# Loading values by head over all 128 partitions, with the keys of a block taken in the order 7u + n

## The chip, the cores and the metric

The kernel runs on one core of one Trainium2 chip. The metric is the device time of one execution in microseconds (us); lower is better.

## The reference

The program is a sigmoid attention followed by a mixture-of-depths layer. Everything is float32. Cut to what matters:

```python
# q, k, v: (B=8, H=12, S=448, Dh=64)
scores = q @ k.T / sqrt(64) - log(448)         # per batch and head, 448 x 448
attn = 1 / (1 + exp(-scores))                  # no softmax: each weight stands alone
x = (attn @ v), heads side by side             # (8, 448, 768)
score = x @ w_gate                             # one number per token
top = the 128 tokens of a batch with the highest score
out = x;  out[top] += sigmoid(score[top]) * (relu(x[top] @ w1) @ w2)   # w1 768 x 1024, w2 1024 x 768
```

Because each attention weight stands alone and the product with v sums over all keys, the keys of a head may be taken in any order, provided that the rows of v are taken in the same order.

## The kernel before

**Tiling.** The 8 x 12 heads are handled in 24 quads of four heads, and two quads make one of the NS = 12 stages s. A head has 448 tokens, seen as 32 groups of TB = 14 consecutive tokens: token 14t + r, with t the partition within a group of 32 partitions and r from 0 to 13. A quad's q or k therefore fills 128 partitions (4 heads x 32 values of t) with 14 x 64 numbers each, and is loaded by one DMA (`load`, L91). VectorE then turns 32 x 32 blocks (`turn`, L367), so that TensorE finds the head dimension on partitions.

**Slots.** Each stage has NU = 7 slots n. In a slot, `score` (L387) forms the scores of 128 keys (64 of either quad) against all 448 queries, `squash` (L402) applies the sigmoid on ScalarE into an `attn` tile, and `value` (L416) multiplies earlier `attn` tiles with `raw_v` and accumulates in PSUM. The scores run ahead of the values: the values of stage s begin in slot 4 of stage s and end in slot 3 of stage s + 1. In stages 4 to 11 a piece of the mixture-of-depths layer (`block`, L736) is placed between slot 3 and slot 4.

**Which keys a slot takes.** A pair of key columns r lies side by side in `kT`. In `turn` the pairs are (n, n + 7). In stage 0 the pairs are others: `load_first` loads columns 3 to 10 of the keys first (AT = 3), `turn_first` turns pairs such as (3, 9) and (5, 7), and `load_second` brings the values and the remaining columns 0 to 2 and 11 to 13.

**Values.** `load_v` (L189) fills `raw_v`: 32 partitions hold, for one quad and for either the even or the odd member of the pairs, seven columns of four heads. So one stage's values come in four DMAs m, each onto 32 partitions, each with 128 pieces of 1,792 bytes:

```python
def block(x, r, n):
    return bass.AP(tensor=v.tensor, offset=v.offset + (8 * s + 4 * x) * S * Dh + r * Dh,
                   ap=[[TB * Dh, TT], [S * Dh, 4], [1, n * Dh]])
```

Stage 0 is loaded in two parts: first five columns (`load_v(0, True)`, L219), then two (`load_v(0, False)`, L222). In front of the first part stands a one-element `memset` of `raw_v` on VectorE (L205). The DMAs wait for it, so its place in VectorE's order sets when SP may issue them. In stages 1 to 5 the values are issued by SP (L216): `after` calls `load_v(s + 1)` at slot 3 of stage s, and `load_v(1)` in slot 6 of stage 0. From stage 6 on they are issued by ScalarE's queue (L216), `load_v(s)` at slot 3 of stage s itself: from stage 7 on the tile is free only when the values of stage s - 1 are finished, and slot 4 needs it. The `block` of the stage lies between.

**Order.** The kernel writes its order out by hand (`stream`, `slot`, `after`); each engine executes its own instructions in that order. SP issues nearly all loads and stores on one queue, ScalarE the late values on a second, GpSimd the small exchanges and the gathers on a third. `raw_k` has one buffer, so each key load waits until VectorE has turned the keys before it.

Of the kernel before, what the change touches and what calls it, by code (L numbers as in the profile page):

```python
# [17 lines left out]
def kernel(  # L18
# [11 lines left out]
    nc = tc.nc  # L30

    B, H, S, Dh = q.shape
# [3 lines left out]
    P = 128  # L36
    TT = 32
    TB = S // TT
# [5 lines left out]
    NU = 2 * NF + 1  # L44
# [44 lines left out]
    heads, raw_v = {}, {}  # L89

    def load(which, *quads):  # L91

        for i in quads:
            if i >= NQ:
                return
            if which == "q":
                t = heads["q", i] = head.tile([P, TB * Dh], F32, name="qT")
            elif i == 2:
                t = heads["both"][:, TB * Dh:2 * TB * Dh]
            else:  # L100
                t = head.tile([P, TB * Dh], F32, name="raw_k", bufs=1)
            src = q if which == "q" else k
            nc.sync.dma_start(
                out=t, in_=bass.AP(tensor=src.tensor, offset=src.offset + i * 4 * S * Dh,
                                   ap=[[TB * Dh, P], [1, TB * Dh]]))
            heads[which, i] = t

    def load_first():

        raw = {}  # L110
        for i in range(2):
            if i:
                both = heads["both"] = moe.tile([P, 6 * KH * P], F32, name="rows_t")
                raw["k", i] = both[:, :TB * Dh]
            else:
                raw["k", i] = head.tile([P, TB * Dh], F32, name="raw_k", bufs=1)
            raw["q", i] = head.tile([P, TB * Dh], F32, name="qT")
            for which, src, at, n in (("k", k, AT, TB - 2 * AT), ("q", q, 0, TB)):
                heads[which, i] = raw[which, i]
                nc.sync.dma_start(  # L120
                    out=raw[which, i][:, at * Dh:(at + n) * Dh],
                    in_=bass.AP(tensor=src.tensor, offset=src.offset + (i * 4 * S + at) * Dh,
                                ap=[[TB * Dh, P], [1, n * Dh]]))

    def load_second():

        load_v(0, True)
        for i in range(2):
            t = heads["k", i].rearrange("p (r d) -> p r d", d=Dh)
            for r in (0, TB - AT):  # L130
                nc.sync.dma_start(
                    out=t[:, r:r + AT],
                    in_=bass.AP(tensor=k.tensor, offset=k.offset + (i * 4 * S + r) * Dh,
                                ap=[[TB * Dh, P], [Dh, AT], [1, Dh]]))
        load_v(0, False)

    turned = {}

    def turn_first(i, *parts):

        t = heads["k", i].rearrange("p (r e d) -> p e r d", e=2, d=TT)
        if i not in turned:
            turned[i] = head.tile([P, 2, TB, TT], F32, name="kT")
        kt = turned[i]
        for part in parts:
            if part < 2:
                nc.vector.transpose(kt[:, :, 2 * part:2 * part + 2],
                                    t[:, :, AT + part:AT + part + NA + 2:NA + 1])
                nc.vector.transpose(kt[:, :, 2 * (NA + part):2 * (NA + part) + 2],
                                    t[:, :, NA + part:NA + part + 3:2])  # L150
                continue
            for a, r in ((0, 0), (1, TB - AT)):
                nc.vector.transpose(kt[:, :, 4 + a:2 * NA:2], t[:, :, r:r + AT])  # L153

    def spare(n):
        return spares.tile([P, QW], F32, name=f"spare{n}")
# [6 lines left out]
    def chunks(s, n, y):  # L163

        if s:
            return y, n, NU
        alone = n < 2 if y else 1 < n < 4
        if alone:
            return 1 - y, 2 * NA + n % 2, 2
        return y, n - 2 * (y or n > 3), NA  # L170

    def column(s, n, y):

        x, c, step = chunks(s, n, y)
        return c if s or step == NA else c - NA

    NA = NU - 2
    AT = NA - 2
    assert NA + 4 + NA == TB and AT + 8 + AT == TB

    hiddens = {}

    def hidden(p):

        if p not in hiddens:
            hiddens[p] = moe.tile([P, 7 * FH * P], F32, name="hidden")
        return hiddens[p]

    def load_v(s, pairs_too=None):  # L189


        if s >= NS:
            return
        if s == 0 and not pairs_too:
            t = raw_v[s]
        elif s in (1, 3):
            t = moe.tile([P, 6 * KH * P], F32, name="rows_t")[:, :4 * NU * Dh]
        elif s == min(BLOCKS) + 1:
            t = hidden(0)[:, 3 * FH * P:3 * FH * P + 4 * NU * Dh]
        else:  # L200
            t = vals.tile([P, 4 * NU * Dh], F32, name="raw_v")
        if s or pairs_too:
            raw_v[s] = t = t.rearrange("p (h c) -> p h c", h=4)
        if pairs_too:
            nc.vector.memset(t[:1, 0, :1], 0.0)  # L205

        def block(x, r, n):
            return bass.AP(tensor=v.tensor,
                           offset=v.offset + (8 * s + 4 * x) * S * Dh + r * Dh,
                           ap=[[TB * Dh, TT], [S * Dh, 4], [1, n * Dh]])  # L210

        for m in range(4):
            y, odd = divmod(m, 2)
            rows = slice(m * TT, (m + 1) * TT)
            if s:
                (nc.scalar if s > 5 else nc.sync).dma_start(  # L216
                    out=t[rows], in_=block(y, odd * NU, NU))
            elif pairs_too:
                nc.sync.dma_start(out=t[rows, :, :NA * Dh],  # L219
                                  in_=block(y, odd * (NA + 4), NA))  # L220
            else:
                nc.sync.dma_start(out=t[rows, :, NA * Dh:],  # L222
                                  in_=block(1 - y, NA + 2 * odd, 2))

    QW = KH * FH * P
    assert D == 4 * NF * Dh and 4 * NU * Dh <= 6 * KH * P
# [138 lines left out]
    def turn(which, *quads):  # L367


        for i in quads:  # L370
            if i >= NQ:
                return
            t = heads[which, i].rearrange("p (r e d) -> p e r d", e=2, d=TT)
            if which == "q":
                if i > 1:
                    nc.vector.transpose(heads["q", i], heads["q", i])  # L376
                    continue
                heads["q", i] = qt = head.tile([P, TB * Dh], F32, name="qT")
                qt = qt.rearrange("p (e r t) -> p e r t", e=2, t=TT)
                for e in range(2):  # L380
                    nc.vector.transpose(qt[:, e], t[:, e])
                continue
            heads["k", i] = kt = head.tile([P, 2, TB, TT], F32, name="kT")
            for e in range(2):
                nc.vector.transpose(kt[:, e], t[:, e].rearrange("p (a n) d -> p n a d", a=2))  # L385

    def score(s, n, e, pr, out):  # L387

# [27 lines left out]
    def value(s, half, p, n):  # L416


        for r in (2 * half, 2 * half + 1):
            x, c, step = chunks(s, n, half)  # L420
            pr = r % 2 ^ p
            rows = slice(r * TT, (r + 1) * TT)
            at = column(s, n, half)
            if s == 0 and at < NA and r % 2 == 0:
                at = (at + AT) % NA
            at *= Dh
            i = done[s, x, pr] = done.get((s, x, pr), 0) + 1
            for j in range(2):
                nc.tensor.matmul(PO[x][pr][j * Dh:(j + 1) * Dh, :S],  # L429
                                 raw_v[s][rows, 2 * pr + j, at:at + Dh],  # L430
                                 attn[s, pr, n][rows, j, :],
                                 start=((s, x, pr, j) not in done), stop=(i == TB))
                done[s, x, pr, j] = True
# [539 lines left out]
    def after(s, n):  # L973

        if n == NF and s:
            odd = s in FULL[1::2]
# [31 lines left out]
            lend(m, key, place)  # L1008
        if s == 0:
            if n == 0:  # L1010
                turn_first(1, 0)
                load_second()
                turn("q", 1)
                turn_first(1, 1)
                turn_first(0, 2)
                turn_first(1, 2)
                load("k", 2, 3)
                load("q", 2, 3)
            if n == 4:
                turn("k", 2, 3)  # L1020
                gate_weights()
                load("k", 4)
            if n == 5:
                turn("q", 2, 3)
            if n == 6:
                load_v(1)
        if (s, n) in WEIGHTS:
            m, x = WEIGHTS[s, n]
# [81 lines left out]
```

## Time and profile before

| | |
|---|---|
| Median of 3 runs | 434.03 us (432.82 to 434.27) |
| The profiled execution | 434.43 us, of which the span of the profile is 432.6 us and 1.8 us lie around it |
| TensorE busy | 424.7 us (98%) |
| VectorE, ScalarE, GpSimd busy | 281.6, 190.3, 48.0 us |
| DMA moved | 78.64 MB in 114,937 packets, mean 182 GB/s |
| Granted TensorE clock | 1.0 |

The profile gives, for each engine, its busy time; the span in 40 slices with a digit in tenths; the DMA queues with packets, bytes and the share of the time of all 16 DMA engines together; and, by query, who waited for whom and single instructions in order of time. Queue q1 is SP's, q10 is ScalarE's and q0 is GpSimd's. PE is TensorE, DVE VectorE, ACT ScalarE, POOL GpSimd. A busy share of the DMA is a mean over 16 DMA engines: it does not say how evenly they are loaded.

### The profile page before, as it was taken

How to read it: one execution, taken by the hardware profiler on the slowest of the kernel's cores; microseconds unless marked ns; L12 is line 12 of the kernel's file. 1: busy time of each engine (PE TensorE's matmuls, PEld its weight loads, DVE VectorE, ACT ScalarE, POOL GpSimd, SP SyncE). 2: the span in 40 equal slices, each digit the busy share in tenths (PEclk: the TensorE clock that was granted, in tenths of full speed). 3: DMA queues.
4: the chain of work that ended last, by engine and by line, in shares of the span. 5: the costliest groups of instructions: out<-in, count | busy, mean ns of one | idle time of the engine just before them, and what ended most of it. 6: DMA issues, size and time to landing. Idle time of an engine off the chain costs nothing.

```text
span 432.6 us, 14250 instructions
## 1 busy us (share of the span) xinstructions
PE 424.7 (98%) x6324; PEld 254.7 (59%) x6324; DVE 281.6 (65%) x597; ACT 190.3 (44%) x249; POOL 48.0 (11%) x81
## 2 busy tenths in 40 slices
PE   8999999999999999999999999999999999999995
PEld 3455453545666478465447549546545859769952
DVE  4427557583967776976968636755666648983472
ACT  4666656666664633650660651563264330101100
POOL 3000001210210020100302020010020110101001
PEclk9999999999999999999999999999999999999999
DMA  6896747899863997988566887399935981821001
GB/s 191 245 273 178 285 89 155 207 209 251 252 180 74 244 296 186 261 269 204 182 224 184 240 204 152 103 265 277 264 109 116 236 241 36 162 57 77 23 1 73
DMA packets 114937, 78.64 MB, mean 182 GB/s; under 512 B 91420, under 2 KB 100892, under 8 KB 114876
## 3 DMA queue, kind: packets, MB, share of 16 engines
q1 hardware_dynamic: 107948, 62.47, 55.0%
q0 software_dynamic: 3296, 9.54, 7.6%
q10 hardware_dynamic: 3632, 5.74, 5.4%
q8 instruction: 49, 0.80, 0.8%
q14 instruction: 12, 0.10, 0.1%
HBM read 57.25 MB, written 20.48 MB: 180 GB/s over the span
## 4 chain that ended last, share of the span: by engine, by line
PE 93%; DMA 3%; ACT 1%; issue 1%; SPq 1%; DVE 1%; POOLq 0%; ACTq 0%
PE a L397 30%; PE o L429 28%; PE o L616 11%; PE o L680 11%; PE a L616 6%; PE a L680 5%; DMA rows_t<-in_k_dram 1%; DMA raw_k<-in_k_dram 1%; PE o L580 1%; ACT attn L411 1%; DMA out_dram<-xe,idx 1%; SPq L219 0%; PE a L580 0%; POOLq L1105 0%; SPq L120 0%
## 5 line engine op out<-in xcount | busy, mean ns | idle before, releaser
L397 PE MATMUL a<-qT,kT 32*64 32x448 f32 x2624 | 244.9, 537 | 0.9 <-DVE kT L153 0.5
L411 ACT ACTIVATE attn<-a,bias_s 128x896 f32<-128x896 f32 x162 | 161.4, 1007 | 86.1 <-PE a L397 81.7
L429 PE MATMUL o<-attn,raw_v 32*64 32x448 f32 x1952 | 176.6, 537 | 0.1
L397 PEld LDWEIGHTS a<-qT,kT 32*64 32x64 f32 x2624 | 95.6, 131 | 90.3 <-ACT attn L411 52.8
L429 PEld LDWEIGHTS o<-attn,raw_v 32*64 32x64 f32 x1952 | 69.5, 131 | 29.3 <-issue 22.5
L453 DVE STREAM_TRANSPOSE x_b<-o 128x448 f32<-128x448 f32 x48 | 28.1, 626 | 53.6 <-PE o L429 37.3
L429 PE MATMUL o<-attn,rows_t 32*64 32x448 f32 x448 | 41.9, 538 | 0.0
L632 ACT ACTIVATE hidden<-hidden 128x512 f32<-128x512 f32 x12 | 7.5, 630 | 65.8 <-DVE hidden L629 65.8
L629 DVE TENSOR_TENSOR hidden<-o,hidden 128x512 f32<-128x512 f32 x23 | 15.2, 687 | 24.2 <-PE o L616 24.0
L464 DVE TENSOR_REDUCE gate_p<-scr 128x14 f32<-128x448 f32 x48 | 29.8, 621 | 1.7
L461 DVE TENSOR_TENSOR scr<-x_b,wg_b 128x448 f32<-128x448 f32 x48 | 29.5, 615 | 1.1
L385 DVE STREAM_TRANSPOSE kT<-raw_k 128x448 f32<-128x448 f32 x42 | 24.1, 611 | 4.0 <-PE a L397 3.7
L376 DVE STREAM_TRANSPOSE qT<-qT 128x896 f32<-128x896 f32 x22 | 23.8, 1083 | 4.2 <-DMA qT<-in_q_dram 3.5
L616 PE MATMUL o<-rows_t,spare 128*128 128x128 f32 x216 | 25.6, 276 | 0.0
L616 PEld LDWEIGHTS o<-rows_t,spare 128*128 128x128 f32 x216 | 24.8, 192 | 1.4 <-DVE x_b L453 1.4
L680 PE MATMUL o<-spare,hidden 128*128 128x384 f32 x72 | 24.3, 487 | 0.0
L691 DVE SCALAR_TENSOR_TENSOR xe<-o,gate,xe 128x384 f32<-128x384 f32 x29 | 16.6, 612 | 9.7 <-PE o L680 9.6
L519 DVE SCALAR_TENSOR_TENSOR scr<-rep,who,tie 128x448 f32<-128x448 f32 (+1 forms) x28 | 18.9, 677 | 4.9 <-DMA rep<-scores 4.2
L535 POOL DMA_DIRECT2D ranks<-turned x28 | 14.5, 525 | 67.0 <-DVE turned L532 67.0
L429 PEld LDWEIGHTS o<-attn,rows_t 32*64 32x64 f32 x448 | 17.0, 131 | 5.7 <-issue 5.2
L429 PE MATMUL o<-attn,hidden 32*64 32x448 f32 x224 | 20.2, 535 | 0.0
L616 PEld LDWEIGHTS o<-rows_t,w_sb 128*128 128x128 f32 x168 | 19.3, 192 | 1.0 <-DVE x_b L453 0.7
(118 smaller groups left out, 392.7 us busy)
## 6 DMA issues: line engine op xcount, KB each, us to landing
qT<-in_q_dram SPq DMA_DIRECT2D x24, 448.0 KB
out_dram<-x_b SPq DMA_DIRECT2D x32, 336.0 KB
raw_k<-in_k_dram SPq DMA_DIRECT2D x21, 448.0 KB
spare<-sum SPq DMA_DIRECT2D x18, 384.0 KB
sum<-spare SPq DMA_DIRECT2D x8, 768.0 KB
raw_v<-in_v_dram ACTq DMA_DIRECT2D x24, 224.0 KB
w_sb<-in_moe_w_dram SPq DMA_DIRECT2D x6, 768.0 KB
rows_t<-in_v_dram SPq DMA_DIRECT2D x8, 224.0 KB
```

The source lines that it names most:

```text
L376: nc.vector.transpose(heads["q", i], heads["q", i])
L385: nc.vector.transpose(kt[:, e], t[:, e].rearrange("p (a n) d -> p n a d", a=2))
L397: nc.tensor.matmul(out[y * Dh:(y + 1) * Dh, h % 2, :S], kt[d, e, r:r + 2].rearrange("d r t -> d (r t)"), qt[d, e], start=(e == 0), stop=(e ...
L411: nc.scalar.activation(a, psc[:, :, :S], AF.Sigmoid, bias=bias_s, scale=QK_SCALE)
L429: nc.tensor.matmul(PO[x][pr][j * Dh:(j + 1) * Dh, :S], raw_v[s][rows, 2 * pr + j, at:at + Dh], attn[s, pr, n][rows, j, :], start=((s, x, p ...
L453: nc.vector.transpose(x_tiles[b][:, :, 2 * g + pr, :], PO[x][pr][:, :S].rearrange("p (r t) -> p r t", t=TT))
L461: nc.vector.tensor_tensor(out=tmp, in0=x_tiles[b][:, :, hp, :], in1=wg_b[:, hp:hp + 1, :].to_broadcast([P, TB, TT]), op=ALU.mult)
L464: nc.vector.tensor_reduce(out=gate_parts[b][:, :, hp], in_=tmp, axis=AX.X, op=ALU.add)
L519: nc.vector.scalar_tensor_tensor(out=junk[:n], in0=rep[:n], scalar=own, in1=tie[:n], op0=ALU.subtract, op1=ALU.is_gt, accum_out=place_s[:n ...
L616: nc.tensor.matmul(ps[:, f, :n], w((t * FH + f) * P, P), x[:, t, :n], start=(t == 0), stop=(t == KH - 1))
L680: nc.tensor.matmul(ps[:n, :DH], h[:, t, :n], w(t * DH, DH), start=(t == 0), stop=(t == FH - 1))
L691: nc.vector.scalar_tensor_tensor(out=xe[:n, cols], in0=ps[:n, :DH], scalar=st[b]["gate"][:n, 0:1], in1=xe[:n, cols], op0=ALU.mult, op1=ALU ...
```

## The change

1. **Values.** A stage's values are now laid out by key order 7u + n: token 7u + n of a head lies on partition u (64 partitions for each of the two quads) in column n. `load_v` issues one DMA for each of the four heads, onto 128 partitions. The pieces are again 1,792 bytes. On the DRAM side the pattern is two quads, then 64 rows, then 448 numbers; on the SBUF side it is 128 partitions, then 448 numbers. The built program carries them so: `[114688, 2], [448, 64], [1, 448]` against `[1792, 128], [1, 1], [1, 448]` (stride, count). Before, both sides began with a count of 32. For stage 0 the first part has the same form with 320 numbers; the second part is two DMAs of 64 partitions.
2. **Turns of k.** To match, the two members of a pair are interleaved key by key: `by_two` makes each turn of k write with a stride of two numbers.
3. **First keys.** Stage 0 now uses the pairs (n, n + 7) as well. `first_keys` loads columns 3 to 6 and 10 to 13 first (two pieces of 1,024 bytes for each partition, before one of 2,048), then columns 0 to 2 and 7 to 9 in one DMA a quad (before two).
4. **Order.** `load_second` stands before `turn_first(1, 0)` instead of after it. On VectorE the `memset` of `raw_v` comes before the two turns of the second quad's first keys. On SP `load_second` has 8 DMAs instead of 12. The instructions of TensorE, ScalarE and GpSimd keep their number and order, and so do all other DMAs.

```diff
+    def first_keys(i, r, n):
+        t = heads["k", i].rearrange("p (a c) -> p a c", a=2)
+        nc.sync.dma_start(
+            out=t[:, :, r * Dh:(r + n) * Dh],
+            in_=bass.AP(tensor=k.tensor, offset=k.offset + (i * 4 * S + r) * Dh,
+                        ap=[[TB * Dh, P], [NU * Dh, 2], [1, n * Dh]]))
...
     def load_second():
         load_v(0, True)
         for i in range(2):
-            t = heads["k", i].rearrange("p (r d) -> p r d", d=Dh)
-            for r in (0, TB - AT):
-                nc.sync.dma_start(
...
+            first_keys(i, 0, AT)
         load_v(0, False)
...
+    def by_two(t):
+        return t.rearrange("p e (n a) t -> p e n (a t)", a=2).rearrange(
+            "p e n (t a) -> p e n a t", a=2)
...
-        for m in range(4):
-            y, odd = divmod(m, 2)
-            rows = slice(m * TT, (m + 1) * TT)
-            if s:
-                (nc.scalar if s > 5 else nc.sync).dma_start(
-                    out=t[rows], in_=block(y, odd * NU, NU))
...
+        def rows(x, h, n, *dims):
+            return bass.AP(tensor=v.tensor,
+                           offset=v.offset + (8 * s + 4 * x + h) * S * Dh + n * Dh,
+                           ap=[*dims, [NU * Dh, 2 * TT]])
+
+        if s or pairs_too:
+            n = NU if s else NA
+            for h in range(4):
+                src = rows(0, h, 0, [4 * S * Dh, 2])
+                src = bass.AP(tensor=src.tensor, offset=src.offset, ap=[*src.ap, [1, n * Dh]])
+                (nc.scalar if s > 5 else nc.sync).dma_start(out=t[:, h, :n * Dh], in_=src)
+            return
+        for y in range(2):
+            src = rows(1 - y, 0, NA)
+            src = bass.AP(tensor=src.tensor, offset=src.offset,
+                          ap=[*src.ap, [S * Dh, 4], [1, 2 * Dh]])
+            nc.sync.dma_start(out=t[y * Dh:(y + 1) * Dh, :, NA * Dh:], in_=src)
...
-                nc.vector.transpose(kt[:, e], t[:, e].rearrange("p (a n) d -> p n a d", a=2))
+                nc.vector.transpose(by_two(kt)[:, e], t[:, e].rearrange("p (a n) d -> p n a d", a=2))
...
             if n == 0:
+                load_second()
                 turn_first(1, 0)
-                load_second()
                 turn("q", 1)
```

More of the change, by code (lines that the diff above doesn't have):

```diff
@@ L116, in load_first @@
                 raw["k", i] = head.tile([P, TB * Dh], F32, name="raw_k", bufs=1)
+            heads["k", i] = raw["k", i]
             raw["q", i] = head.tile([P, TB * Dh], F32, name="qT")
-            for which, src, at, n in (("k", k, AT, TB - 2 * AT), ("q", q, 0, TB)):
-                heads[which, i] = raw[which, i]
-                nc.sync.dma_start(
-                    out=raw[which, i][:, at * Dh:(at + n) * Dh],
-                    in_=bass.AP(tensor=src.tensor, offset=src.offset + (i * 4 * S + at) * Dh,
-                                ap=[[TB * Dh, P], [1, n * Dh]]))
+            first_keys(i, AT, NU - AT)
+            t = heads["q", i] = raw["q", i]
+            nc.sync.dma_start(
+                out=t, in_=bass.AP(tensor=q.tensor, offset=q.offset + i * 4 * S * Dh,
+                                   ap=[[TB * Dh, P], [1, TB * Dh]]))
     def load_second():
@@ L128, in load_second @@
         for i in range(2):
-            t = heads["k", i].rearrange("p (r d) -> p r d", d=Dh)
-            for r in (0, TB - AT):
[L131 to L134, printed above, removed]
+            first_keys(i, 0, AT)
         load_v(0, False)
@@ L139, in turn_first @@
     def turn_first(i, *parts):
-        t = heads["k", i].rearrange("p (r e d) -> p e r d", e=2, d=TT)
+        t = heads["k", i].rearrange("p (a n e d) -> p e n a d", a=2, e=2, d=TT)
         if i not in turned:
             turned[i] = head.tile([P, 2, TB, TT], F32, name="kT")
-        kt = turned[i]
+        kt = by_two(turned[i])
         for part in parts:
             if part < 2:
[L147 to L150, printed above, removed]
+                for at, n in ((part, AT + part), (NA + part, NA + part)):
+                    nc.vector.transpose(kt[:, :, at], t[:, :, n])
                 continue
-            for a, r in ((0, 0), (1, TB - AT)):
-                nc.vector.transpose(kt[:, :, 4 + a:2 * NA:2], t[:, :, r:r + AT])
+            for a in range(2):
+                nc.vector.transpose(kt[:, :, 2:NA, a], t[:, :, :AT, a])
+    def by_two(t):
+        return t.rearrange("p e (n a) t -> p e n (a t)", a=2).rearrange(
+            "p e n (t a) -> p e n a t", a=2)
     def spare(n):
@@ L178 @@
     AT = NA - 2
-    assert NA + 4 + NA == TB and AT + 8 + AT == TB
+    assert NA + 2 == NU and AT + 4 == NU and TB == 2 * NU
     hiddens = {}
@@ L205, in load_v @@
             nc.vector.memset(t[:1, 0, :1], 0.0)
-        def block(x, r, n):
+        def rows(x, h, n, *dims):
             return bass.AP(tensor=v.tensor,
-                           offset=v.offset + (8 * s + 4 * x) * S * Dh + r * Dh,
-                           ap=[[TB * Dh, TT], [S * Dh, 4], [1, n * Dh]])
-        for m in range(4):
-            y, odd = divmod(m, 2)
-            rows = slice(m * TT, (m + 1) * TT)
-            if s:
-                (nc.scalar if s > 5 else nc.sync).dma_start(
-                    out=t[rows], in_=block(y, odd * NU, NU))
[L218 to L223, printed above, removed]
+                           offset=v.offset + (8 * s + 4 * x + h) * S * Dh + n * Dh,
[12 more added lines that the diff above has]
+            nc.sync.dma_start(out=t[y * Dh:(y + 1) * Dh, :, NA * Dh:], in_=src)
     QW = KH * FH * P
@@ L423, in value @@
             at = column(s, n, half)
-            if s == 0 and at < NA and r % 2 == 0:
+            if s == 0 and at < NA:
                 at = (at + AT) % NA
```

## The prediction

> **What bounds the kernel now.** First the busy table and the slices of the page:
>
> ```profile
> span 432.6 us, 14250 instructions
> PE 424.7 (98%) x6324; PEld 254.7 (59%) x6324; DVE 281.6 (65%) x597; ACT 190.3 (44%) x249; POOL 48.0 (11%) x81
> ...
> DMA  6896747899863997988566887399935981821001
> ...
> q1 hardware_dynamic: 107948, 62.47, 55.0%
> ...
> q10 hardware_dynamic: 3632, 5.74, 5.4%
> ```
>
> TensorE is busy 98% of the span: any gain must come from its 8 us of idle time, and a loss comes from any load that arrives late. The DMA digits say that the 16 engines are far from idle while values are loaded. By stretches (PE, PEld, DVE, ACT, POOL, then clock, DMA share, GB/s):
>
> ```profile
> 6.70:104.00 97.30, 96.68 (x1913) 47.46 (x1895) 53.25 (x122) 64.05 (x76) 6.86 (x11) 1.00 0.80 209
> ...
> 155.00:346.00 191.00, 190.66 (x2800) 114.70 (x2806) 131.01 (x268) 83.54 (x116) 21.44 (x33) 1.00 0.78 205
> ```
>
> The DMA engines are 0.80 and 0.78 busy there, evenly loaded or not, and TensorE still waits for none of them: all loads fit their windows. How wide the windows are, the timeline shows; here stage 9, first ScalarE's queue, then TensorE:
>
> ```profile
> 260.20 0.32 ACTq L216 DMA_DIRECT2D raw_v<-in_v_dram  x1
> ...
> 262.04 0.95 ACTq L216 DMA_DIRECT2D raw_v<-in_v_dram  x2
> ```
>
> ```profile
> 273.26 0.60 PE L397 MATMUL a<-qT,kT 32*64 32x448 f32 x4
> 273.28 0.60 PE L429 MATMUL o<-attn,raw_v 32*64 32x448 f32 x4
> ```
>
> From the first issue to the first use: 13.1 us. Read in the same way, the windows of stages 6 to 11 are 13.0 (155.16 to 168.18), 13.5 (190.81 to 204.32), 10.4 (226.34 to 236.72), 13.1, 13.5 (295.34 to 308.85) and 11.0 (330.85 to 341.88), mean 12.4 us. The DMA view of 256 to 285 us gives what one stage's values cost:
>
> ```profile
> q10 hardware_dynamic: 576, 0.92, 13.3%
> ```
>
> That is 0.133 x 16 x 29 us = 62 us of one engine, or 3.9 us on each of 16. The view of 30 to 35 us shows the pace of a saturated DMA:
>
> ```profile
> DMA  9999989989999999999999999999897637000000
> GB/s 430 401 401 459 459 344 459 459 344 402 430 459 393 397 410 406 373 422 373 410 410 393 442 426 393 393 426 360 328 344 295 246 131 213 16 0 0 0 0 0
> ```
>
> About 410 GB/s at a digit of 9, or 25.7 GB/s for each engine.
>
> **What the skill says.** (1) "DMA: Bandwidth & Descriptors", section "Why a DMA increments its semaphore by 16 and not by 1": a DMA is cut along the slowest dimension with a count over 1 of each side, over the largest number k of engines, at most 16, that divides both counts; each used engine adds one completion write; from SP and ScalarE the lowest-numbered k engines are taken. The trace agrees as far as it can. Queue q10 has 3,632 packets. The code puts on it 24 value DMAs of 128 pieces (3,072), one of 128 rows (128) and four of 4 rows (16): 3,216. The remaining 416 are 25 x 16 + 4 x 4, so a 4-row DMA used 4 engines; had it used 16, there would be 464. That the engines are the lowest ones no run here shows yet. (2) Same page, "Queues, rings and completion order": each engine works a queue's pieces in ring order and takes turns between queues. (3) "SBUF — State Buffer", "Door 1: The DMA port swizzle": 32 partitions reach half of the 16 ports. The trace fits: the values ran at 0.92 MB in 62 us, 15 GB/s for each engine, against 25.7. (4) Same page, same section: SBUF works in lines of 16 bytes and needs two hits in each, so a stride of two 4-byte numbers should be free. No strided turn is in the trace.
>
> **The change, part by part.**
>
> *Values, the part that decides.* The DRAM side now begins with a count of 2 and the SBUF side with 128. By (1), k = 2: every value DMA runs on the same two engines. A set of four is 917,504 bytes, 35.7 us of an engine at 25.7 GB/s, so at least 17.9 us on two. At the old pace of 15 to 17.6 GB/s (10.9% of 16 x 30 us between 150 and 180) it would be 26 to 31 us. Now each half of the partitions has its own ports, so I take the fast end with some cost for pieces: **19 us a set** instead of 3.9, and 13.6 us for stage 0's first part (655,360 bytes).
>
> Over the run: without the values the engines work about 220 us each between 6.7 and 346 us (shares of .80, .75 and .78 by their stretches of 97.3, 51 and 191 us, 265 us, less 45 for 11.7 sets). Two engines then get 220 + 11 x 19 + 14 = 443 us of work in 339 us. They become the bound: +104 us if they never rest, some 30 less if the other pieces run faster once they are no longer in each other's way.
>
> *Where that shows, early.* Stage 0: values issued at 7.16 us were used at 13.11. Issued near 6.4 and begun behind the second q load, near 7.5, they land at 7.5 + 13.6 + about 1.5 = 22.6 us, so TensorE stands for 9 us. The second keys are behind them in SP's ring, and all later loads behind those. In stages 1 to 4 a set takes 19 us of a 22 us stage, with keys, queries, stores and weights queued behind it. VectorE waits for keys before it can empty PSUM. Up to the landing of stage 5's values: 13.6 + 5 x 19 = 109 us, plus other loads of 39 us (209 GB/s x 97.3 us less 4.3 MB of values, at 25.7 GB/s an engine) to 61 us (0.80 x 97.3 less 17 for 4.7 sets). From 6.7 us this ends at 155 to 177; they were needed at 134.4. So +21 to +43; I take **+35**, stage 0's 9 us included, as the two engines sometimes rest.
>
> *Late.* Stages 6 to 11 load inside a window of 12.4 us, with nothing to start earlier. A set needs 19 us, about 2 us of issue and landing (an exchange of 1.8 KB between 55 and 75 us takes 1.8), and turns with the other queues: none to 8 us (0.9 of the window less 3.5 for the values); I take 4. That is 25 us, 12.6 late, **six times: +76 us** (8.6 to 16.6 each: +52 to +100). ScalarE's sequencer[...] may delay the copies of `block` (L582, L635) queued behind L216; that lies in the same wait and is costed at 0 to 3 us a stage, 0 taken.
>
> *Turns of k.* 42 at 611 ns (L385) and 12 smaller ones. At no extra cost by (4); if a strided write took twice as long, 26 us more on VectorE, which is idle for 150 us. Its cover is that idle time; in the waits it would add up to 10 us. A gain has no reason. 0 taken.
>
> *First keys and order.* The memset moves ahead of two turns (0.31 and 0.27 us) and of their wait for the second keys (0.38): from 7.07 to about 6.3 us. Moved with it are four value, two key and two value DMAs; past SP nothing else changes place. Four issues fewer save 4 x 0.45 us of SP. The first keys in 256 pieces instead of 128 cost an estimated 0.1 us (eight more for each engine). The second q load, landing at 7.69, may meet the first values and come up to 1 us later. Without the k = 2 effect this gives -1.5 to +1 us: TensorE waited 0.5 us for the late keys' turn (L153), little more is to be had. Under k = 2 it drowns. 0 taken.
>
> Sum: 434.4 + 35 + 76 = 545 us on the profiled execution, whose own time stands 0.4 us over the median; the forecast is **545 us**.
>
> **Rivals.** *All 16 engines after all (the other side).* If the split follows the 128 partitions, a set goes over all ports: 35.7 / 16 = 2.2 us instead of 3.9, and every window keeps its room. Then only the head gains: 0.5 us at L153 and up to 1 us of earlier values: 433 us (432 to 435). For it: both sides walk 128 rows and the change's wording. Against it: (1) and the 416 packets. It decides from about k = 4: 35.7 / 4 + 2 = 11 us just fits the windows. *Two engines, but other ones for each DMA.* Four DMAs on eight engines: 4.5 us a set plus 2, hidden; about 436 us. Against it is the page's "lowest-numbered". *Two engines at the old pace.* If 1,792-byte pieces keep 15 to 17.6 GB/s, a set takes 26 to 31 us: about 8 us more for each of 11.7 sets, 545 + 94 = 639 us. Against it: ports no longer shared.
>
> **How the numbers follow.** k = 2 on the same engines 0.88 (0.06 of it at the old pace), all 16 0.08, different pairs 0.04. The k = 2 case itself: low, 434 + 21 + 52 - 13 (17.9 for 19, 11.7 sets) = 494; high, 434 + 43 + 100 + 18 (ScalarE) + 10 (turns) = 605, and up to 639 at the old pace. The range 490 to 625 holds about 0.82; the cases near 434 are left out. A difference within 0.3% is what a measurement of this kernel cannot tell from none. Faster: half of the all-16 case, 0.04. Same: 0.05. Slower: 0.91.
>
> **What would show it.** q10 should have 24 x 14 = 336 packets fewer, 3,296, if two engines write completions, and the same number if 16. The window view should show 520 packets on q10 a set. TensorE's weight loads at L429 should wait for DMA `raw_v` at every stage from 6 on, by 9 to 17 us, and at about 13 us in stage 0; TensorE should fall under 80% busy; the DMA digits should show long runs of 1 and 2 where only two engines work. The turns at L385's place should stay near 611 ns. If q10 keeps 3,632 packets and TensorE 98%, the prediction is wrong at its first step; if the waits are there with another length, the pace of 19 us is.

## The result, and the profile after

The changed kernel takes 595.86 us (median of 4 runs, 594.32 to 596.97), against 433.94 us before on the same chip: ratio 1.3735, 95% interval 1.3693 to 1.3777, so 162 us slower. The forecast was 545 us, in a range of 490 to 625. Times here and below are medians of all executions; in e8 and e10 one slow execution each (564.32 and 599.97 us) is left out of the ratio and its interval.

The page of the changed kernel, with the lines that answer to those of before (busy table, slices of TensorE, its clock and the DMA, queues):

```profile
span 594.7 us, 14229 instructions
PE 474.4 (80%) x6324; PEld 273.1 (46%) x6324; DVE 281.9 (47%) x597; ACT 191.2 (32%) x249; POOL 47.8 (8%) x81
...
PE   8796939995945995399489639959947974999996
...
PEclk9697977997986998599779859989987995999999
DMA  3625263646653896336406553449462163525201
...
q1 hardware_dynamic: 107804, 62.47, 38.6%
...
q10 hardware_dynamic: 3296, 5.74, 2.6%
```

The same bytes move, and the DMA is less busy than before, although the kernel now waits for it. Queue q10 has 3,296 packets: the 24 value DMAs have two completion packets each instead of 16, the number forecast to the packet. TensorE has lost its even row of nines, and the clock row, all nines before, now dips; that was not forecast.

The chain that ended last names the bound (share of the span by engine):

```profile
PE 45%; DMA 37%; DVE 5%; ACTq 5%; SPq 4%; issue 3%; ACT 1%; POOLq 0%; DVEq 0%
```

Before, TensorE held 93% of it and the DMA 3%. Two waits stand out, one for the late stages and one for the early ones (engine and line, waited for, us in total, times, longest):

```profile
PE o L432 <- DMA raw_v<-in_v_dram: 72.7, 18, 8.9
...
DVE kT L388 <- DMA raw_k<-in_k_dram: 57.5, 6, 15.6
```

TensorE's `value` (L432 here, L429 before) waits for values, and VectorE's `turn` (L388, before L385) waits for keys that stand behind values in SP's queue. Such a stand, time in which an engine only waits, looks like this on TensorE in stage 6, where the values were first issued at 214.25 us (idle time before an instruction is in brackets):

```profile
229.37 0.93 PE L432 MATMUL o<-attn,raw_v 32*64 32x448 f32 x2 [1.16 <-DMA raw_v<-in_v_dram]
234.63 1.75 PE L432 MATMUL o<-attn,raw_v 32*64 32x448 f32 x2 [4.33 <-DMA raw_v<-in_v_dram]
243.26 1.72 PE L432 MATMUL o<-attn,raw_v 32*64 32x448 f32 x2 [6.88 <-DMA raw_v<-in_v_dram]
249.25 1.00 PE L432 MATMUL o<-attn,raw_v 32*64 32x448 f32 x1 [4.27 <-DMA raw_v<-in_v_dram]
```

The heads come one after the other, 5 to 9 us apart: the four DMAs of a set do not run side by side. The DMA view of 440 to 452 us (stage 10) shows how few engines work meanwhile:

```profile
DMA  9997311111110111111111111111111111110000
GB/s 381 381 446 299 147 53 65 44 53 51 63 53 41 44 53 65 44 44 53 65 49 41 48 55 54 49 48 54 55 48 49 48 49 48 49 60 24 0 0 0
```

A digit of 1 at 49 GB/s is two engines of 16 (0.125) at 24.5 GB/s each. From 424 to 452 us the same set reads:

```profile
q10 hardware_dynamic: 520, 0.92, 8.9%
```

That is 0.089 x 16 x 28 = 40 us of one engine, 20 us on two; before, the set was 62 us of one engine in stage 9, spread over 16. So a set now costs a third less engine time, but five times as long on the engines that carry it. That the layout over 128 partitions makes the pieces cheaper does not follow; the run with three engines below speaks against it.

### The profile page after: what moved, and what is told of

It reads as the page before. It is cut to its first block, busy times and chain, and to the rows that moved or that the text cites. A ratio compares the mean times of both kernels' runs of the same rounds, so it can differ in the third digit from the quotient of the medians.

```text
span 594.7 us, 14229 instructions
## 1 busy us (share of the span) xinstructions
PE 474.4 (80%) x6324; PEld 273.1 (46%) x6324; DVE 281.9 (47%) x597; ACT 191.2 (32%) x249; POOL 47.8 (8%) x81
## 3 DMA queue, kind: packets, MB, share of 16 engines
q0 software_dynamic: 3296, 9.54, 5.2%
q10 hardware_dynamic: 3296, 5.74, 2.6%
## 4 chain that ended last, share of the span: by engine, by line
PE 45%; DMA 37%; DVE 5%; ACTq 5%; SPq 4%; issue 3%; ACT 1%; POOLq 0%; DVEq 0%
DMA raw_v<-in_v_dram 23%; PE o L432 16%; PE a L400 16%; PE o L619 5%; ACTq L222 5%; DMA raw_k<-in_k_dram 4%; PE o L683 4%; DMA rows_t<-in_v_dram 3%; DMA qT<-in_q_dram 3%; DMA spare<-in_moe_w_dram 2%; PE a L619 2%; PE a L683 2%; SPq L222 2%; DMA rows_t<-in_k_dram 1%; SPq L103 1%
## 5 line engine op out<-in xcount | busy, mean ns | idle before, releaser
L400 PE MATMUL a<-qT,kT 32*64 32x448 f32 x2624 | 273.0, 578 | 3.4 <-ACT hidden L638 3.3
L432 PE MATMUL o<-attn,raw_v 32*64 32x448 f32 x1952 | 212.0, 576 | 78.4 <-DMA raw_v<-in_v_dram 68.5
L400 PEld LDWEIGHTS a<-qT,kT 32*64 32x64 f32 x2624 | 107.1, 140 | 100.4 <-ACT attn L414 47.9
L432 PEld LDWEIGHTS o<-attn,raw_v 32*64 32x64 f32 x1952 | 79.4, 142 | 125.9 <-DMA raw_v<-in_v_dram 59.1
L388 DVE STREAM_TRANSPOSE kT<-raw_k 128x448 f32<-128x448 f32 x42 | 24.3, 620 | 110.6 <-DMA raw_k<-in_k_dram 57.5
L456 DVE STREAM_TRANSPOSE x_b<-o 128x448 f32<-128x448 f32 x48 | 27.6, 621 | 80.8 <-PE o L432 62.0
L432 PE MATMUL o<-attn,rows_t 32*64 32x448 f32 x448 | 44.6, 553 | 5.8 <-DMA rows_t<-in_v_dram 5.8
L444 ACT ACTIVATE o<-bias_s 1x1 f32<-1x1 f32 x40 | 5.3, 157 | 86.7 <-PE a L400 69.2
L619 PE MATMUL o<-rows_t,w_sb 128*128 128x128 f32 x168 | 21.7, 291 | 14.2 <-DVE x_b L456 14.2
L619 PEld LDWEIGHTS o<-rows_t,w_sb 128*128 128x128 f32 x168 | 21.2, 207 | 15.2 <-DVE x_b L456 15.0
L432 PEld LDWEIGHTS o<-attn,rows_t 32*64 32x64 f32 x448 | 16.0, 135 | 14.1 <-issue 7.9
```

The source lines that it names most:

```text
L388: nc.vector.transpose(by_two(kt)[:, e], t[:, e].rearrange("p (a n) d -> p n a d", a=2))
L400: nc.tensor.matmul(out[y * Dh:(y + 1) * Dh, h % 2, :S], kt[d, e, r:r + 2].rearrange("d r t -> d (r t)"), qt[d, e], start=(e == 0), stop=(e ...
L432: nc.tensor.matmul(PO[x][pr][j * Dh:(j + 1) * Dh, :S], raw_v[s][rows, 2 * pr + j, at:at + Dh], attn[s, pr, n][rows, j, :], start=((s, x, p ...
L456: nc.vector.transpose(x_tiles[b][:, :, 2 * g + pr, :], PO[x][pr][:, :S].rearrange("p (r t) -> p r t", t=TT))
L619: nc.tensor.matmul(ps[:, f, :n], w((t * FH + f) * P, P), x[:, t, :n], start=(t == 0), stop=(t == KH - 1))
```

## Experiments

Each difference is to runs of the kernel before that were timed beside the experiment.

**One part at a time: which stages lose how much.** Where a stage is to use 16 engines, its values come as two DMAs of 64 partitions, so that both sides begin with a count of 64; nothing else is changed. The edit in `load_v`, with the condition that each run sets:

```diff
+        if (s or pairs_too) and (s > 5):       # e1; "s < 6" in e2, "s > 0" in e3, True in e5
+            n = NU if s else NA
+            for y in range(2):
+                src = rows(y, 0, 0)
+                src = bass.AP(tensor=src.tensor, offset=src.offset,
+                              ap=[*src.ap, [S * Dh, 4], [1, n * Dh]])
+                (nc.scalar if s > 5 else nc.sync).dma_start(
+                    out=t[y * Dh:(y + 1) * Dh, :, :n * Dh], in_=src)
+            return
```

> The changed kernel, but the values of stages 6 to 11 come as two DMAs of 64 partitions and four heads (both sides begin with a count of 64: 16 engines); stages 0 to 5 keep four DMAs on two engines. Theory (two engines): only the early part of the loss is left. In the changed kernel the values of stage 5 were first used 57.6 us later than before, so 434 + 58 = 492 us (480 to 500), with 3,632 - 24 x 16 + 12 x 16 = 3,440 packets on ScalarE's queue. Rival (the late windows alone make the loss, and early lateness is absorbed by them): 434 to 445 us.

> The reverse: stages 0 to 5 over 16 engines, stages 6 to 11 on two. Theory: only the late part is left, 6 stages of 16.9 us as the two traces show it (160.7 us at stage 11's values less 59.1 at stage 6's issue), 434 + 102 = 536 us (520 to 545); and the two parts add up to the whole 162 us within 10 us. Rival (a backlog from the early stages is what makes the late loads slow, so that late alone costs only 6 x 8.6): 485 us.

> Only stage 0's first part of the values is on two engines, all later stages on 16. Theory: the stand of stage 0 alone, 9 us, plus one or two for a cold TensorE clock: 444 us (441 to 448). Rival (the head's delay is taken back by slack in stages 1 to 3): 435 us.

Measured: 492.91, 539.21 and 443.76 us, with 431.72 before: +61.2, +107.5 and +12.0 us (ratios 1.1419, 1.1395 to 1.1443; 1.2501, 1.2417 to 1.2584; 1.0274, 1.0246 to 1.0302). Early and late add up to 168.7, against 162 for the whole, within the 10 us allowed. Each part is a loss of its own: the early lateness is not absorbed, and the late one needs no backlog from the early stages. Stage 0 alone costs 12 us.

**All stages on 16 engines (e5), and the place of load_second (e6).** In e6 `turn_first(1, 0)` stands before `load_second()` again.

> The changed kernel with every stage's values as two DMAs of 64 partitions and four heads, so on 16 engines; key order, strided turns, first keys and the early place of load_second stay as changed. Theory: the engine count is the whole loss, and the rest of the change is worth what the rival of the forecast gave it: 433 us where the kernel before has 434, that is a ratio of 0.995 to 1.002, with 3,632 - 12 x 16 = 3,440 packets on ScalarE's queue. Rival (strided turns or the new first loads also cost): 1.005 or more.

> As the one before, but load_second stands behind turn_first(1, 0) again, as in the kernel before. Theory: the place is worth the 0.76 us by which the values are issued earlier, at most, as TensorE waited 0.5 us for the late keys: 0 to 1 us slower than with the early place. Rival (the early values meet the second q load and delay it): up to 1 us faster than with the early place.

Measured: 433.40 us for e5 and 434.94 us for e6, with 432.15 before; ratios 1.0022 (1.0005 to 1.0040) and 1.0068 (1.0042 to 1.0094). So the form of the value DMAs is 99% of the loss; that it is the number of engines in it, the next run shows. The rest of the change gains nothing: with it the kernel stands 1.3 us over the kernel before. With the later place it is slower by another 1.5 us, more than the 0 to 1 expected, though the two intervals (0.2 to 1.7 and 1.8 to 4.1 us over the kernel before) only just lie apart. No run here beats the kernel before, and none loads values onto 128 partitions with 16 engines, so what the layout alone is worth stays open. In e5's profile q10 has the expected 3,440 packets, TensorE is back at 98%, and the set costs about what it did in the old layout:

```profile
q10 hardware_dynamic: 544, 0.92, 12.9%
```

That is 60 us of one engine between 256 and 285 us, as against 62: with 64 partitions instead of 32 a piece is no cheaper while 16 engines write. Over the whole run q10 takes 5.5% of the engines' time, against 5.4% before.

**Three engines instead of two (e4).** Both quads' 64 partitions are cut into 51 and 13:

```diff
+            for y in range(2):
+                for a, m in ((0, 51), (51, 13)):
+                    src = bass.AP(tensor=v.tensor,
+                                  offset=v.offset + (8 * s + 4 * y) * S * Dh + a * NU * Dh,
+                                  ap=[[NU * Dh, m], [S * Dh, 4], [1, n * Dh]])
```

> All stages' values cut otherwise: for each quad one DMA of 51 partitions and one of 13, four heads each. By the rule of the largest divisor up to 16, the first runs on 3 engines and the second on 13. Same pieces of 1,792 bytes, same bytes, same 64 partitions of a quad. Theory: 408 pieces on 3 engines at 74 ns and 8 on each of 13: 10.7 us a set instead of 19, so 17 to 20 us from issue to landing against a window of 12.4: 5 to 8 us a stage late, about 4 to 10 us early: 434 + 45 = 479 us (460 to 500). Rival (what hurts is the leading count of 2 or the 128-partition form, not the number of engines): within 3 us of the kernel before.

Measured: 494.08 us, +62.4 (ratio 1.1410, 1.1330 to 1.1491), inside the range, 15 us over the 479 expected. The rival falls: no side begins with 2 here, no DMA has 128 partitions, and yet 51 rows, which no number from 4 to 16 divides, cost 62 us. The count of packets on q10 agrees: 3,440 = 3,216 + 12 x (3 + 13) + 16 + 4 x 4. The surplus is early: its stage 6 is issued at 185.92 us, 31 late where 4 to 10 were expected, and VectorE waits 26.6 us for keys at its turns. Even with room to spare on an engine over a whole stage, keys stand behind a burst of values.

The same run tells more about the cheaper pieces. From 351.5 to 356.5 us almost nothing but 51-row DMAs of stage 10 is moving:

```profile
DMA  2131212212121212121221212122121212122121
...
q10 hardware_dynamic: 195, 0.34, 17.8%
```

The 17.8% are 2.8 engines of 16, and 0.34 MB in 0.178 x 16 x 5 = 14.2 us of one engine is 24 GB/s for each, although the 51 partitions of a DMA lie within one half. That is the pace of the changed kernel, 24.5 GB/s; so it goes with few engines at work and needs no 128 partitions.

**The same DMAs, other engines (e8).** Stages 1 to 5 from GpSimd's queue:

```diff
-                (nc.scalar if s > 5 else nc.sync).dma_start(out=t[:, h, :n * Dh], in_=src)
+                (nc.scalar if s > 5 else nc.gpsimd if s else nc.sync).dma_start(out=t[:, h, :n * Dh], in_=src)
```

> The changed kernel, but the values of stages 1 to 5 are issued by GpSimd's queue instead of SP's, in the same four DMAs with a leading count of 2. The Trainium skill (DMA: Bandwidth & Descriptors, section Why a DMA increments its semaphore by 16 and not by 1) says that GpSimd's DMAs take k engines in turn, where SP's take the lowest. Theory (the loss comes from all four DMAs of a set, and all later loads, standing in the rings of the same two engines): a set now runs on several pairs, some 5 us instead of 19, and keys no longer wait behind it, so the early part of 61 us shrinks to the 12 of stage 0: 432 + 12 + 108 = 552 us (545 to 565). Rival (a DMA cut in two is slow on any engines, or GpSimd takes the same two): 580 to 600 us.

Measured: 556.28 us, +122.2 (ratio 1.2817, 1.2793 to 1.2842), 42 us less than the changed kernel timed beside it (598.40). The early part shrinks as expected. From issue to landing these DMAs took a median of 9.8 and 10.8 us, where some 5 had been expected for a set (KB each, us):

```profile
rows_t<-in_v_dram POOLq DMA_DIRECT2D x8, 224.0 KB, 10.8
raw_v<-in_v_dram POOLq DMA_DIRECT2D x8, 224.0 KB, 9.8
```

And VectorE's wait for keys, 57.5 us in the changed kernel, is:

```profile
DVE kT L388 <- DMA raw_k<-in_k_dram: 4.7, 2, 2.8
```

So DMAs cut in two are bearable here; in SP's queue ahead of the keys, all on one pair of engines, they are not. By the packets of the trace each DMA is still cut in two, and up to eight packets of a set run at a time: four pairs. But three pieces now travel in one packet of 5,376 bytes. The run moves three things at once, the engines, the queue and the packets, and does not say which of them weighs most.

**The clock (e7, e9, e10).** Matmuls that compute nothing needed fill TensorE's stand in stages 6 to 10:

```diff
             u(0, 1)
+            for _ in range({6: 20, 7: 12, 8: 17, 9: 7, 10: 13}.get(s, 0)):
+                nc.tensor.matmul(PO[1][1][:, :512], iden, w1_sb[:, 0, :512],
+                                 start=True, stop=True)
             value(s, 0, 0, 0)
```

> The changed kernel, with matmuls of no use (128x512, identity against a weight tile, into a bank that the values open later) put before the first values of stages 6 to 10: 20, 12, 17, 7 and 13 of them, about as long as TensorE stands there. The loads are untouched, outputs too. Theory (the stand lets the granted clock fall to half, and the 4 us after it run at half speed): TensorE comes out of the wait at full clock and 1 to 2 us a stage are saved, 5 to 10 us of 596. Rival (the half clock is hidden by the next wait): no change, or slower by what the extra matmuls overrun the wait.

Measured: 593.09 us, ratio 1.3725 (1.3655 to 1.3794). The changed kernel's 1.3735 lies within that interval, so nothing follows. Both were timed again side by side:

> The changed kernel as it is, beside the next run on the same chip: 592 to 597 us. It gives the base that the run with the extra matmuls needs, which was timed in another call than the changed kernel.

> The kernel with extra matmuls in the stand of stages 6 to 10 once more. In its profile the five stages took 254.6 us from stage 6's first issue to stage 11's, against 260.4 in the changed kernel's. Theory (half clock after a stand costs 1 to 2 us a stage): 4 to 8 us below the changed kernel of the same call. Rival (the 5.8 us are scatter of single executions): within 2 us of it.

Measured: 598.40 us without and 591.59 us with the extra matmuls; ratios 1.3787 (1.3757 to 1.3818) and 1.3620 (1.3572 to 1.3668). The intervals are apart: 6.8 us are saved by giving TensorE more to do. The form without them came out 1.4 us over its expected range. In the changed kernel the stretches around the end of stage 6's stand show why (columns as before; the eighth is the granted clock):

```profile
214.25:249.30 35.05, 18.42 (x125) 12.95 (x123) 23.81 (x46) 2.31 (x7) 2.68 (x4) 0.76 0.63 165
249.30:253.50 4.20, 4.20 (x48) 1.67 (x56) 0.00 (x0) 1.17 (x2) 0.00 (x0) 0.53 0.43 77
253.50:258.00 4.50, 4.50 (x97) 2.52 (x89) 0.00 (x0) 2.53 (x3) 0.00 (x0) 1.00 0.00 0
```

For 4.2 us after the last head landed, the clock was 0.53 and 48 matmuls were done; the next 4.5 us at full clock did 97. The Trainium skill ("TensorE: Matmul & The Clock Gate", section "Part 1: The HAM clock gate (the "warmup" mystery)") says that about 3.4 us without work halve the clock and about 3.4 us of work restore it. The 4.2 us here are of that size, and from 205 to 505 us the mean clock is 0.85 in e9 and 0.97 in e10.

## Why the prediction was right, and where it was off

*The whole: the mechanism was right, the total was in its range partly by luck.* The early part came to 59 us against a stated 21 to 43, the late one to 102 against 52 to 100; both lie outside. With 43 and 100 the sum would be 577, and 596 fell inside only because the range also held room for ScalarE, slower turns and the old pace. Of these the turns and the old pace did not occur, and no run shows ScalarE's share apart.

*k = 2, all on the same two engines: right, and shown.* 3,296 packets on q10; digits of 1 at 49 GB/s; heads landing one by one; +1.3 us once the count is 64; e4 for three engines. The packets of the trace show the pair also in SP's queue. Of the 128 pieces of the key load issued at 128.89 us, 112 started from 135.3 to 137.8 us, while the values of stage 4, issued before it, were still running two at a time. The other 16, the share of two engines in sixteen, started only at 142.2 us, when these values were nearly through. That is also the ring order of point (2). That the two are the lowest-numbered engines no run shows.

*19 us a set: right.* 40 us of an engine, 20 on two. The price was taken near the pace of full ports rather than the old 15 to 17.6 GB/s, and the trace has 24.5 GB/s. The reason given for it, own ports for each half of the partitions, is not borne out: e4 has the same pace within one half. The number was right with luck.

*Early, +35: the term that was too small.* Stage 5's values were first used at 191.93 us. Before, that was at 132.83 us; the 134.4 of the forecast is a later matmul of the same values:

```profile
132.83 0.61 PE L429 MATMUL o<-attn,hidden 32*64 32x448 f32 x4
```

So the delay is 59.1 us; e1 gives 61.2 for the part. By the packets of the trace these values had landed at 177.3 us, and the forecast's sum of work for the two engines ended at 155 to 177 (in it "less 17 for 4.7 sets" should read 18): the landing was at its upper end, so the two engines rested less than the +35 allowed for. The step that failed comes after it. The forecast set the landing against the first use and put nothing between them, and 15 us lay between. From 152 to 192 us the DMA reads, one digit for each microsecond:

```profile
DMA  9995201111111145499999941111199986830000
```

The second run of 1, at 176 to 181 us, is values only at its start. Then the two engines work off their share of keys and weights issued behind them. VectorE waits for both, and only then empties PSUM (L456):

```profile
178.94 1.17 DVE L388 STREAM_TRANSPOSE kT<-raw_k 128x448 f32<-128x448 f32 x2 [15.62 <-DMA raw_k<-in_k_dram]
180.73 1.76 DVE L276 TENSOR_TENSOR spare<-spare,w_sb 128x1536 f32<-128x1536 f32 x1 [0.62 <-DMA spare<-in_moe_w_dram]
...
183.80 2.23 DVE L456 STREAM_TRANSPOSE x_b<-o 128x448 f32<-128x448 f32 x4
```

TensorE waits for that, has a piece of the mixture-of-depths layer next in its order, and reaches the values after it:

```profile
184.50 7.48 PE L619 MATMUL o<-rows_t,w_sb 128*128 128x128 f32 x48 [14.21 <-DVE x_b L456]
```

From 188 to 192 us the DMA had nothing left to do. The forecast named this path, through keys and PSUM, but gave it no time. VectorE in stage 3 shows it too:

```profile
143.91 1.17 DVE L388 STREAM_TRANSPOSE kT<-raw_k 128x448 f32<-128x448 f32 x2 [14.49 <-DMA raw_k<-in_k_dram]
145.00 2.20 DVE L456 STREAM_TRANSPOSE x_b<-o 128x448 f32<-128x448 f32 x4
```

Stage 0, 9 us forecast, was 12 (e3): its heads came at 19.3 and 22.8 us, the latter against 22.6 forecast, and the matmuls after that ran at a clock of 0.50 until 28 us.

*Late, +76: 102 us* (stage 11's first values 160.7 us late, less stage 6's first issue 59.1 us late; e2, with this part alone, 107.5). The six times from first issue to the value matmul that follows the last landing were 35.0, 26.4, 29.5, 21.8, 28.1 and 27.6 us, mean 28.1 against 25 forecast; less the six windows of 74.5 us, 94 us. What is left for sharing with other queues, beside 19 for the set and 2 for issue and landing, is 7 us on average where 4 was taken. That is within the stated 0 to 8; stage 8 is just over it (8.5), and stage 6 is far over it (14). There ScalarE's sequencer was also held so long that two activations of the block began at 231.00 us only:

```profile
218.43 12.53 ACTq L222 DMA_DIRECT2D raw_v<-in_v_dram  x3
...
231.00 1.15 ACT L635 ACTIVATE hidden<-hidden 128x512 f32<-128x512 f32 x2 [15.76 <-DVE kT L388]
```

That was costed at 0 to 3 us a stage with 0 taken; no run shows it apart. The other 8 us of the 102 fit the half clock after each stand, which the forecast did not have at all: e10 gives 6.8 for five of the six stages.

*Turns of k, 0: right.* With its stride of two numbers L388 took 620 ns a turn against 611 of L385, as point (4) had it. *First keys and order: near.* Together with the rest, e5 puts them at +1.3 us, where -1.5 to +1 stood. Where it goes is open: SP's four first issues took 2.46 us in e5 against 1.67 in the profile of the kernel before, and the first query turn began at 5.10 instead of 4.68 us, but a part of the 1.3 is within the interval's width.

*The rivals.* All 16 engines, 433 us: falls for the change. When the count was made 64, its 433 was met in number (433.40), but the gain of about 1 us that it stood for did not come: the kernel before took 432.15 beside it. Different pairs for each DMA falls for SP's and ScalarE's queues, where the values ran two packets at a time. The old pace falls, with 24.5 GB/s.

## What to carry to other kernels

Before a load is reshaped, look at the first count above 1 on both of its sides, not at the number of partitions: in these runs it decided how many engines moved it, and a leading 2 cost 162 us, a 51 still 62, while no gain from the wider layout was seen. When some engines carry more than others, the mean DMA share hides it; compare completion packets, and look for long runs of a low digit. Reckon a late load not by its own landing alone: loads behind it in its queue are late too, the engines that wait for those do their work only then, and the matmuls after each stand are slow.

## What the runs showed of the hardware that was not expected

- A stand of TensorE costs more than its length: after it, some 4 us at clock 0.53. Filling the stand of five stages with useless matmuls made the kernel 6.8 us faster (591.59 against 598.40).
- Issuing can itself take long when values run on two engines: ScalarE's three last issues of stage 6 took 12.5 us, four of SP at 47.87 us took 17.5, against 1.8 for four at 36.71 us before. What holds them no run shows.
- A load over 16 engines issued behind values on two is split in time: 112 of the 128 pieces of a key load started from 135.3 to 137.8 us, the last 16 only at 142.2 us.
- Values over 64 partitions and 16 engines (e5) cost 60 us of an engine for a set, as with 32 partitions (62), while over 128 partitions on two engines it was 40. In e4, with 3 and 13 engines, it was 44 in stage 10 (9.8% of 16 x 28 us between 344 and 372 us), within one half of the partitions at a time.
